# New lists for every queue of a fused attention and gMLP kernel: another order of the last early x, and other distances between scores, maximum and shift

## The chip, the cores and the metric

The kernel runs on one core of one Trainium2 chip. A time is device microseconds of one execution; of several runs the median is given. The core has five engines that work beside each other, each strictly through its own queue: TensorE (PE, with its weight loads PEld), VectorE (DVE), ScalarE (ACT), GpSimd (POOL) and SyncE (SP), which here issues nearly all transfers. They wait for each other through semaphores only.

## The reference

```python
def _attn_ref(q, k, v, tau):              # (8, 8, 576, 64) each
    scale = 1.0 / np.sqrt(q.shape[-1])
    scores = scale * np.matmul(q, k.transpose(0, 1, 3, 2))
    thresh = np.max(scores, axis=-1, keepdims=True) - tau
    scores = np.where(scores >= thresh, scores, -1000000000.0)
    scores = scores - np.max(scores, axis=-1, keepdims=True)
    attn = np.exp(scores)
    attn = attn / (np.sum(attn, axis=-1, keepdims=True) + 1e-09)
    return np.matmul(attn, v)

def _moe_ref(x, w_in, w_spatial, b_spatial, w_out):    # x: (8, 576, 512)
    h = np.maximum(x @ w_in, 0.0)
    u, v = h[..., :512], h[..., 512:]
    v_n = (v - mean(v)) / np.sqrt(var(v) + 1e-06)      # over the last axis
    v_s = np.einsum('ts,bsd->btd', w_spatial, v_n) + b_spatial[None, :, None]
    return (u * v_s) @ w_out
```

The attention of all heads is laid side by side as x and goes through the gMLP. Only scores within tau = 0.02 of their row's maximum keep a weight.

## The kernel before

**Steps.** The 64 heads form 32 pairs of two heads of one batch. The 576 rows of a pair are four blocks of 128 and one of 64; the two blocks of 64 of neighbouring pairs share a step. That gives 18 steps a batch and 144 in all. Step g uses bank g % 2 of the two score banks `s_ring`, slot g % 3 of `e_ring`, g % 10 of `p_ring` and g % 12 of `pT_ring`. So the scores of step g + 2 cannot start before the exponentials of step g have left the bank.

**Tokens.** Nothing chooses the order while the kernel is built: `ORDER` holds one list of tokens for each of eight rounds, `LAST` four short lists for the end. `run_token` reads them one by one and emits each one's instructions. Since every engine takes its own in order, a list fixes five queues at once; the order between two tokens of different engines matters only by what their data needs. `S14:0` is step 14 of the round's own batch; `:1` means the batch before, `:2` two before, `:-1` the next.

One step, with the line where each works and its engine:

- `S` (`scores`, line 817, PE): most of the scores. `G` (`turn_bank`): an empty instruction that waits for one of them, on GpSimd, or on ScalarE (`aG`) or VectorE (`vG`). `Y` (`scores_end`, PE): the rest of the scores, which waits for `G`.
- `M` (`top`, line 851, DVE): the row maximum of both heads. `B` (`shift`, line 857, DVE): it becomes a bias that has tau in it.
- `E`, `F` (`spread`, lines 872 and 875, ACT): one head each, out of the bank.
- Then the step's way in `WAYS`. Way a: `E` and `F` give the shifted scores, with those below the threshold driven far down, and `Z` (`exps`, line 910, ACT) the exponential of both heads. Way n: `E` and `F` give the exponential, `C` (`keep`, line 894, DVE) the mask and `A` (`pick`, line 903, DVE) the masked numerator.
- `T` (`turn_p`, line 915, SP): a DMA transpose of the numerators p into pT.

Other tokens: `Pmjk` (PE) is one step's product of pT and v, three of them fill a bank; `imj` (line 532, DVE) takes the reciprocal of the sums and `pmj` (line 535, DVE) writes x. `X0` and `X1` (`send_x`, line 556, SP) transpose the x of two pairs by DMA into xT; `XP` and `xp` do it on TensorE with an eviction. `v`, `u`, `s`, `o` (lines 643, 710, 739, 768, PE) are the gMLP's products and `ev`, `bv`, `eu`, `es`, `eo` evict them; `bs` and `ba` or `n` and `k` make statistics, `N` the norm (lines 683 to 695, GpSimd); `OUT` (lines 700 and 787) stores. `QA`, `QB`, `QR` transpose q and k on PE, `qa`, `qb`, `qr` evict them, `kd`, `sq`, `sv` copy on GpSimd, `L` loads. A `d` ahead of an eviction puts it on VectorE instead of ScalarE.

```python
        elif kind in ("X", "XR"):
            send_x(m, 4 if kind == "XR" or 2 * m in x_on_pe else 0, 5 if kind == "XR" else 9)
```

**The end.** After round 7 the score banks are given up for six more banks, and `LAST[1]` finishes batch 6's gMLP and batch 7's attention. `X0:1` there sends the early x of batch 7, from its steps 0 to 8; the late x goes through `XP2` and `XP3`. Then `last_gmlp` runs batch 7's gMLP: its first products (line 935) need all of xT; bn_stats (line 944), the norm, the gate (line 983) and the output (line 1002) follow. `LAST[2]` and `LAST[3]` put its u products between.

Of the kernel before, what the change touches and what calls it, by code (L numbers as in the profile page):

```python
# [11 lines left out]
F16 = mybir.dt.float16  # L12
# [8 lines left out]
    "S0:0 L8:0 aG0:0 Y0:0 QA1:0 qa1:0 L6:-1 M0:0 S1:0 G1:0 Y1:0 QR1:0 L7:0 B0:0 F0:0 sk1:0 M1:0 B1:0 E0:0 "  # L21
    "QB1:0 C0:0 S2:0 A0:0 qb1:0 Cb0:0 aG2:0 E1:0 Y2:0 M2:0 B2:0 F1:0 Z1:0 S3:0 dqr1:0 G3:0 Y3:0 F2:0 E2:0 "
    "L4:-1 sv0:0 QR2:0 kd1:0 S4:0 G4:0 M3:0 Y4:0 B3:0 E3:0 F3:0 Z3:0 S5:0 C2:0 G5:0 Y5:0 sq2:0 QA2:0 A2:0 "
    "Ci1:0 M4:0 B4:0 M5:0 E4:0 F4:0 S6:0 B5:0 C4:0 vG6:0 E5:0 A4:0 F5:0 Y6:0 S7:0 G7:0 M6:0 Z5:0 Y7:0 qr2:0 "
    "sv1:0 sq3:0 QB2:0 B6:0 T0:0 kd2:0 M7:0 F6:0 E6:0 Cbs0:0 S8:0 B7:0 vG8:0 qa2:0 E7:0 F7:0 dqb2:0 Y8:0 "
    "RP01:0 M8:0 Z6:0 S9:0 vG9:0 Y9:0 T2:0 B8:0 F8:0 C7:0 E8:0 L1:-1 QR3:0 rp01:0 S10:0 G10:0 qr3:0 M9:0 "
    "L3:-1 Y10:0 B9:0 E9:0 kd3:0 F9:0 RP00:0 Cis1:0 A7:0 M10:0 L0:-1 T1:0 Z8:0 S11:0 sq0:-1 vG11:0 L9:0 T3:0 "
    "T6:0 B10:0 F10:0 Y11:0 QB3:0 drp00:0 M11:0 QA3:0 E10:0 S12:0 Co0:0 qb3:0 G12:0 Y12:0 T5:0 C9:0 qa3:0 "
    "B11:0 QB0:-1 F11:0 A9:0 sq1:-1 E11:0 M12:0 S13:0 G13:0 Y13:0 B12:0 P000:0 P001:0 C11:0 M13:0 B13:0 T7:0 "
    "P002:0 Z10:0 A11:0 F12:0 E12:0 S14:0 qb0:-1 aG14:0 Y14:0 P010:0 M14:0 P011:0 i00:0 F13:0 Cs1:0 B14:0 "  # L30
    "E13:0 S15:0 p00:0 Css2:0 G15:0 Y15:0 P012:0 Z12:0 QR0:-1 M15:0 i01:0 B15:0 T8:0 E14:0 F14:0 sv3:0 S16:0 "
    "dqr0:-1 G16:0 T9:0 Z14:0 L7:-1 T11:0 F15:0 sv2:0 p01:0 Y16:0 kd0:-1 QA0:-1 M16:0 P020:0 E15:0 Z13:0 "
    "P021:0 S17:0 C15:0 B16:0 dqa0:-1 aG17:0 Y17:0 E16:0 P100:0 P022:0 A15:0 T10:0 F16:0 Z16:0 M17:0 "),
(
    "S0:0 i02:1 G0:0 B17:1 Y0:0 P101:1 p02:1 M0:0 Ci0:1 F17:1 P102:1 RP11:1 i10:1 Cis0:1 E17:1 S1:0 B0:0 "
    "Cos0:1 Z17:1 T14:1 G1:0 Y1:0 p10:1 drp11:1 WS2:1 E0:0 F0:0 QB1:0 S2:0 ws2:1 G2:0 M1:0 Y2:0 QA1:0 B1:0 "
    "E1:0 T12:1 C0:0 L2:0 Css3:1 dqb1:0 F1:0 M2:0 qa1:0 RP10:1 S3:0 G3:0 B2:0 T16:1 Y3:0 QR1:0 rp10:1 A0:0 "
    "P110:1 P111:1 F2:0 dqr1:0 M3:0 P112:1 kd1:0 T15:1 E2:0 S4:0 vG4:0 Y4:0 Z1:0 B3:0 i11:1 P120:1 p11:1 M4:0 "
    "L9:0 T17:1 P121:1 B4:0 F3:0 P122:1 E3:0 S5:0 G5:0 Y5:0 i12:1 XP1:1 Z2:0 p12:1 M5:0 E4:0 XP0:1 F4:0 L5:0 "
    "L8:0 S6:0 sq2:0 xp1:1 XR0:1 aG6:0 B5:0 Y6:0 QB2:0 dxp0:1 sv0:0 F5:0 Ci2:1 Cis2:1 Ci3:1 M6:0 E5:0 Z3:0 "  # L40
    "XP3:1 S7:0 G7:0 dqb2:0 Y7:0 B6:0 XP2:1 dxp2:1 M7:0 L1:-1 B7:0 xp3:1 Cis3:1 QA2:0 T1:0 E6:0 v0:1 F6:0 "
    "Cs0:1 Z4:0 S8:0 XR1:1 dqa2:0 G8:0 bv0:1 bs0:1 Y8:0 QR2:0 sq3:0 F7:0 dqr2:0 M8:0 v1:1 kd2:0 E7:0 ba0:1 "
    "B8:0 C6:0 S9:0 Z5:0 ev1:1 G9:0 Y9:0 v2:1 L3:-1 F8:0 M9:0 Co1:1 A6:0 B9:0 v3:1 E8:0 Css1:1 S10:0 vG10:0 "
    "bv2:1 bv3:1 C8:0 n1:1 Y10:0 QA3:0 bs3:1 Css0:1 F9:0 E9:0 T2:0 M10:0 WS0:1 S11:0 G11:0 L4:-1 T0:0 Y11:0 "
    "Z7:0 T5:0 T7:0 B10:0 dws0:1 qa3:0 N0:1 M11:0 F10:0 E10:0 QB3:0 u3:1 A8:0 qb3:0 S12:0 G12:0 Y12:0 B11:0 "
    "eu3:1 QR3:0 C10:0 bs2:1 Z9:0 u1:1 F11:0 dqr3:0 M12:0 A10:0 kd3:0 E11:0 u0:1 B12:0 deu0:1 S13:0 k1:1 "
    "aG13:0 eu1:1 sv1:0 Y13:0 v4:1 F12:0 P000:0 M13:0 B13:0 ba2:1 E12:0 bv4:1 T6:0 P001:0 P002:0 E13:0 F13:0 "
    "S14:0 vG14:0 i00:0 Y14:0 p00:0 P020:0 P021:0 T8:0 Cos1:1 P022:0 ba3:1 Cs2:1 Css4:1 T3:0 M14:0 Z11:0 "
    "i02:0 S15:0 G15:0 Y15:0 L0:-1 B14:0 RP00:0 L2:-1 p02:0 E14:0 N3:1 M15:0 F14:0 drp00:0 RP01:0 Z13:0 S16:0 "
    "G16:0 Y16:0 QR0:-1 bs4:1 rp01:0 dqr0:-1 B15:0 WS3:1 Z12:0 sq0:-1 M16:0 ws3:1 P010:0 E15:0 P011:0 P012:0 "  # L50
    "ba4:1 T9:0 QB0:-1 N2:1 Co2:1 i01:0 p01:0 B16:0 F15:0 C14:0 WS1:1 dqb0:-1 E16:0 T10:0 S17:0 aG17:0 kd0:-1 "
    "A14:0 N1:1 Y17:0 QA0:-1 ws1:1 N4:1 M17:0 u2:1 T12:0 F16:0 qa0:-1 T11:0 WS4:1 deu2:1 "),
(
    "S0:0 G0:0 Y0:0 QR1:0 B17:1 Z16:1 dws4:2 M0:0 L7:0 F17:1 E17:1 s1:2 B0:0 es1:2 S1:0 G1:0 Y1:0 sq1:0 Z15:1 "
    "T14:1 qr1:0 E0:0 F0:0 s0:2 Z17:1 M1:0 B1:0 sv3:1 S2:0 T13:1 G2:0 Y2:0 u4:2 es0:2 E1:0 F1:0 M2:0 eu4:2 "
    "QB1:0 B2:0 T16:1 S3:0 sv2:1 qb1:0 G3:0 Y3:0 QA1:0 L8:0 E2:0 F2:0 s2:2 M3:0 qa1:0 T15:1 B3:0 P110:1 kd1:0 "
    "C1:0 S4:0 es2:2 A1:0 G4:0 Y4:0 P111:1 Z0:0 E3:0 F3:0 M4:0 T17:1 L1:-1 sq2:0 P100:1 P112:1 B4:0 S5:0 G5:0 "
    "Y5:0 Cos2:2 P101:1 P102:1 i11:1 p11:1 M5:0 P120:1 T0:0 Z3:0 P121:1 P122:1 E4:0 i10:1 L6:0 F4:0 B5:0 Z2:0 "
    "F5:0 S6:0 G6:0 p10:1 i12:1 Y6:0 L5:0 E5:0 QB2:0 p12:1 sq3:0 Z4:0 M6:0 s3:2 B6:0 S7:0 E6:0 F6:0 Co3:2 "
    "dqb2:0 G7:0 Y7:0 Cos3:2 L9:0 Z5:0 es3:2 QA2:0 XR0:1 XP1:1 S8:0 G8:0 T1:0 M7:0 Y8:0 B7:0 dxp1:1 qa2:0 "  # L60
    "QR2:0 dqr2:0 E7:0 F7:0 X1:1 XP2:1 o3:2 M8:0 kd2:0 xp2:1 C7:0 XP0:1 xp0:1 B8:0 F8:0 T4:0 deo3:2 S9:0 E8:0 "
    "L3:-1 A7:0 G9:0 Z6:0 Y9:0 v0:1 sv1:0 T5:0 S10:0 M9:0 G10:0 B9:0 Y10:0 ev0:1 v2:1 v1:1 C8:0 F9:0 M10:0 "
    "sv2:0 E9:0 bv2:1 T2:0 A8:0 S11:0 B10:0 bv1:1 E10:0 G11:0 n0:1 Y11:0 C9:0 QB3:0 sv0:0 bs2:1 F10:0 bs1:1 "
    "v3:1 qb3:0 Z10:0 QA3:0 S12:0 ba2:1 bv3:1 M11:0 G12:0 Y12:0 QR3:0 ba1:1 B11:0 A9:0 N2:1 M12:0 qa3:0 F11:0 "
    "L0:-1 qr3:0 B12:0 u2:1 E11:0 kd3:0 F12:0 o0:2 E12:0 S13:0 eu2:1 bs3:1 sv3:0 vG13:0 deo0:2 Y13:0 S14:0 "
    "G14:0 Y14:0 s4:2 M13:0 B13:0 T3:0 o1:2 es4:2 T8:0 v4:1 T10:0 T7:0 Z12:0 deo1:2 k0:1 E13:0 F13:0 Z11:0 "
    "S15:0 sq0:-1 N0:1 M14:0 G15:0 bv4:1 Y15:0 ba3:1 L8:-1 u3:1 P000:0 B14:0 P001:0 E14:0 M15:0 P002:0 eu3:1 "
    "F14:0 P010:0 P011:0 P012:0 T6:0 L4:-1 bs4:1 i00:0 N1:1 B15:0 F15:0 E15:0 p00:0 i01:0 QB0:-1 S16:0 G16:0 "
    "L7:-1 p01:0 Y16:0 OUT1:2 u0:1 dqb0:-1 T12:0 ba4:1 QR0:-1 M16:0 deu0:1 S17:0 L9:-1 Z14:0 B16:0 Z13:0 "
    "aG17:0 Y17:0 QA0:-1 qr0:-1 T13:0 N3:1 P020:0 P021:0 M17:0 N4:1 E16:0 qa0:-1 B17:0 P022:0 F16:0 s0:1 "  # L70
    "kd0:-1 C15:0 "),
(
    "S0:0 F17:1 E17:1 Z16:1 T14:1 G0:0 Y0:0 i02:1 S1:0 A15:1 T11:1 L2:0 p02:1 es0:2 M0:0 Z17:1 G1:0 B0:0 Y1:0 "
    "u1:2 X0:1 E0:0 o2:3 T9:1 deu1:2 sq1:0 F0:0 QA1:0 M1:0 sq2:0 S2:0 eo2:3 B1:0 aG2:0 dqa1:0 F1:0 Y2:0 s1:2 "
    "M2:0 B2:0 T16:1 QR1:0 E1:0 es1:2 dqr1:0 Z0:0 OUT3:3 S3:0 G3:0 T15:1 E2:0 Y3:0 T17:1 QB1:0 qb1:0 M3:0 "
    "L0:-1 s2:2 es2:2 s3:2 B3:0 kd1:0 es3:2 Z1:0 P100:1 P101:1 P102:1 F2:0 sq3:0 i10:1 S4:0 G4:0 Y4:0 p10:1 "
    "E3:0 T1:0 F3:0 S5:0 aG5:0 Y5:0 OUT4:3 M4:0 B4:0 P120:1 P121:1 P110:1 M5:0 Z3:0 P111:1 L6:0 P122:1 P112:1 "
    "i12:1 E4:0 F4:0 S6:0 G6:0 L5:0 Y6:0 B5:0 C4:0 p12:1 i11:1 p11:1 M6:0 Z2:0 F5:0 E5:0 o1:2 o0:2 B6:0 S7:0 "
    "G7:0 F6:0 deo1:2 L8:-1 eo0:2 Y7:0 A4:0 QB2:0 o2:2 E6:0 T0:0 L3:-1 qb2:0 sv0:0 M7:0 eo2:2 B7:0 QR2:0 X1:1 "
    "S8:0 L1:-1 qr2:0 G8:0 C5:0 Y8:0 C6:0 QA2:0 T4:0 E7:0 F7:0 qa2:0 v0:1 bv0:1 A5:0 M8:0 T3:0 B8:0 kd2:0 "  # L80
    "S9:0 vG9:0 Y9:0 v1:1 E8:0 F8:0 A6:0 Z7:0 ev1:1 bs0:1 S10:0 M9:0 B9:0 G10:0 F9:0 Y10:0 v3:1 OUT1:2 ba0:1 "
    "v2:1 T6:0 M10:0 C8:0 E9:0 B10:0 C9:0 sv1:0 T7:0 bv3:1 bv2:1 F10:0 sv3:0 S11:0 E10:0 G11:0 Y11:0 A9:0 "
    "u4:2 s4:2 eu4:2 M11:0 sq0:-1 es4:2 A8:0 QB3:0 Z10:0 S12:0 aG12:0 qb3:0 B11:0 F11:0 Y12:0 N0:1 QR3:0 "
    "bs2:1 dqr3:0 E11:0 Z11:0 QA3:0 dqa3:0 T5:0 kd3:0 v4:1 S13:0 G13:0 Y13:0 o3:2 M12:0 B12:0 M13:0 bv4:1 "
    "T2:0 sq1:-1 bs4:1 E12:0 u1:1 sv2:0 B13:0 F12:0 eo3:2 T10:0 S14:0 F13:0 G14:0 Y14:0 deu1:1 P000:0 E13:0 "
# [85 lines left out]
(  # L171
    "u2:1 eu2:1 u3:1 eu3:1 u4:1 eu4:1 ")]
WAYS = [
    "nananaanananaaanaa",
    "naaaaanananaaanaaa",
    "anaaaaannnaaaaanaa",
    "aaaannnannaaaaanaa",
    "aaaaaanaannnaannaa",
    "nnaaannanaanaanaaa",
    "nnaaaanaananaaanaa",  # L180
    "nnaaaanananaaaaaaa",
]

# [1028 lines left out]
```

## Time and profile before

| what | value |
|---|---|
| median of 3 runs | 444.53 us (441.93 to 445.1) |
| the profiled execution | 442.4 us |
| its span, first to last instruction | 440.6 us |
| mean granted TensorE clock | 0.99 |
| PE, DVE, ACT, POOL busy | 412.2, 381.6, 383.1, 169.4 us |
| maxima (line 851) | 144, 1.361 us each |
| E and F (lines 872, 875) | 288 in all, 0.74 us each |
| exponentials of way a (line 910) | 97, 1.172 us each |
| mask and pick of way n (lines 894, 903) | 47, 0.487 and 0.799 us |
| pT transposes (line 915), xT transposes (line 556) | 141 and 15; median to landing 4.4 and 4.8 us |

How to read it: busy is the time in which an engine has at least one instruction in it, so overlapping instructions count once. A matmul's end is modelled, so a PE that is busy all the time still has short waits between groups. A line such as "A <- B: 16.3, 33, 1.4" says that A waited 16.3 us for B in total, 33 times, at most 1.4. The chain of waits goes back from the last instruction to whatever released each one. In the table by stretches, each engine's busy time is followed by its count, then come the granted clock, the share of the DMA engines and GB/s.

### The profile page before, as it was taken

What the parts mean: (1) busy time and instruction counts of PE and PEld (TensorE: products, weight loads), DVE (VectorE), ACT (ScalarE), POOL (GpSimd) and SP (SyncE); (2) the same over time, 40 slices, a digit from 0 to 9 for tenths busy, and PEclk for the clock granted to TensorE, in tenths of its full rate; (3) what the DMA queues carried; (4) which work ended last, traced back from release to release, by engine and by line L of the source; (5) the groups of instructions that cost most, each with busy time, mean ns of one, the idle gap of its engine ahead of it and who ended that gap; (6) DMA issues with size and microseconds to landing.
All of it is one profiled execution on the core that took longest, in us unless ns stands there. A gap on an engine that the chain in (4) does not pass through costs nothing.

```text
span 440.6 us, 12956 instructions
## 1 busy us (share of the span) xinstructions
PE 412.2 (94%) x5048; PEld 256.7 (58%) x5048; DVE 381.6 (87%) x693; ACT 383.1 (87%) x579; POOL 169.4 (38%) x374
## 2 busy tenths in 40 slices
PE   8778888989999999999999999999999999999695
PEld 4445664666656665666665565656656656556352
DVE  6889988898998989998899899889999999995472
ACT  4899999989999888999998998898999988997252
POOL 2254335474346511661137612362155521361021
PEclk9899999999999999999999999999999999999899
DMA  7999999999999999999899999999999997978803
GB/s 199 228 241 214 219 274 190 196 214 209 240 179 239 207 224 230 219 172 207 202 213 187 211 229 189 219 264 235 192 186 188 206 238 152 182 163 135 191 12 109
DMA packets 224637, 88.17 MB, mean 200 GB/s; under 512 B 195648, under 2 KB 220352, under 8 KB 224576
## 3 DMA queue, kind: packets, MB, share of 16 engines
q1 hardware_dynamic: 224048, 86.49, 99.8%
q8 instruction: 40, 0.66, 0.7%
q0 software_dynamic: 160, 0.52, 0.3%
q10 hardware_dynamic: 368, 0.33, 0.2%
q14 instruction: 21, 0.17, 0.2%
HBM read 32.79 MB, written 9.44 MB: 96 GB/s over the span
## 4 chain that ended last, share of the span: by engine, by line
PE 57%; DVE 15%; ACT 13%; DMA 6%; issue 4%; POOL 2%; SPq 0%; POOLq 0%; DVEq 0%; ACTq 0%
PE s L817 23%; DVE s L851 8%; PE f L739 6%; PE f L643 5%; ACT e L875 5%; PE f L497 4%; PE f L710 4%; PE f L435 4%; DMA xT<-xn 4%; PE f L768 3%; ACT p L910 3%; ACT e L872 3%; PE f L492 1%; DVE p L903 1%; DVE xn L535 1%
## 5 line engine op out<-in xcount | busy, mean ns | idle before, releaser
L851 DVE TENSOR_REDUCE s<-s 128x2 f32<-128x1152 f32 x144 | 196.0, 1361 | 17.8 <-PE s L817 15.8
L817 PE MATMUL s<-qkT 64*64 64x160 f32 (+1 forms) x2304 | 173.0, 418 | 10.5 <-ACT e L875 5.3
L817 PEld LDWEIGHTS s<-qkT 64*64 64x64 f32 x2304 | 107.3, 132 | 69.7 <-ACT e L875 16.3
L875 ACT ACTIVATE e<-s,negm 128x576 f32<-128x576 f32 x194 | 134.4, 743 | 10.5 <-DVE negm L857 7.0
L910 ACT ACTIVATE p<-e 128x1152 f16<-128x1152 f32 x97 | 112.5, 1172 | 1.5 <-PE s L817 1.0
L872 ACT ACTIVATE e<-s,negm 128x576 f16<-128x576 f32 x94 | 65.2, 745 | 8.9 <-DVE negm L857 7.6
L321 POOL CAST v<-vl 128x512 bf16<-128x512 f32 x32 | 21.9, 685 | 65.9 <-PE s L817 64.7
L497 PE MATMUL f<-v,pT 128*128 128x65 bf16 x984 | 44.1, 194 | 0.0
L497 PEld LDWEIGHTS <-pT 128*128 128x128 f16 x1024 | 41.8, 98 | 2.0 <-issue 0.5
L903 DVE TENSOR_TENSOR p<-e 128x576 int32<-128x576 int32 x47 | 37.5, 799 | 1.1 <-PE s L817 0.8
L294 POOL COPY qn<-ql 128x512 f32<-128x512 f32 x31 | 20.6, 663 | 42.6 <-PE s L817 42.2
L447 POOL COPY qkT<-qkT 64x64 f32<-64x64 f32 x32 | 8.7, 272 | 67.8 <-ACT qkT L417 33.4
L739 PE MATMUL f<-wsT,vn 128*128 128x512 bf16 x135 | 32.9, 380 | 0.2 <-POOL vn L695 0.2
L710 PE MATMUL f<-xT,w_in 128*128 128x512 bf16 x116 | 29.6, 380 | 0.1
L643 PE MATMUL f<-w_in,xT 128*128 128x512 bf16 x112 | 28.0, 380 | 1.3 <-DMA xT<-xn 1.1
L695 POOL TENSOR_SCALAR vn<-vrel,rs,nm 128x512 bf16<-128x512 f32 (+1 forms) x35 | 27.2, 777 | 3.6
L492 PE MATMUL f<-v,pT 128*128 128x130 bf16 x123 | 27.3, 222 | 1.1 <-DMA pT<-p 0.6
L535 DVE TENSOR_TENSOR xn<-f,r 128x384 bf16<-128x384 f32 x46 | 25.4, 554 | 0.9 <-PE s L817 0.2
L768 PE MATMUL f<-w_o,gT 128*128 128x512 bf16 x100 | 25.4, 380 | 0.3 <-DVE qkT L411 0.2
L857 DVE TENSOR_SCALAR negm<-s 128x2 f32<-128x2 f32 x144 | 22.3, 155 | 3.5 <-PE s L817 0.6
L894 DVE TENSOR_SCALAR e<-e 128x1152 uint16<-128x1152 f16 x47 | 22.8, 487 | 0.3 <-PE s L817 0.2
L739 PEld LDWEIGHTS <-vn 128*128 128x128 bf16 x140 | 12.8, 98 | 15.4 <-issue 2.0
(162 smaller groups left out, 548.4 us busy)
## 6 DMA issues: line engine op xcount, KB each, us to landing
vl<-in_v_dram SPq DMA_DIRECT2D x16, 512.0 KB, 5.6
kl<-in_k_dram SPq DMA_DIRECT2D x15, 512.0 KB, 4.9
ql<-in_q_dram SPq DMA_DIRECT2D x15, 512.0 KB, 5.2
out_dram<-oo SPq DMA_DIRECT2D x12, 512.0 KB, 4.3
pT<-p SPq DMA_TRANSPOSE x141, 4.4
uT<-in_moe_w_in_dram SPq DMA_DIRECT2D x3, 512.0 KB, 5.3
uT<-in_moe_w_spatial_dram SPq DMA_DIRECT2D x2, 576.0 KB, 5.5
vx<-in_v_dram SPq DMA_DIRECT2D x16, 64.0 KB, 4.2
```

The costliest lines, as they stand in the source:

```text
L492: nc.tensor.matmul(out=t[:, at:at + 130], lhsT=pt[:, 4, rows], rhs=vt[:, 4:6, :].rearrange("p b d -> p (b d)"), start=True, stop=False)
L497: nc.tensor.matmul(out=t[:, at + 65 * h:at + 65 * h + 65], lhsT=pt[:, 5 * h + j, rows], rhs=vt[:, 6 * h + j, :], start=False, stop=(h == 1 ...
L643: nc.tensor.matmul(out=t, lhsT=x_of(b, f, slice(c * P, (c + 1) * P)), rhs=w_in[:, f, 512:1024], start=(f == 0), stop=(f == 3))
L710: nc.tensor.matmul(out=t, lhsT=w_in[:, m, f * P:(f + 1) * P], rhs=x_of(b, m, slice(0, 512)), start=(m == 0), stop=(m == 3))
L739: nc.tensor.matmul(out=t, lhsT=vn[:, c, f * P:(f + 1) * P], rhs=wsT[:, c, 0:512], start=(c == 0), stop=(c == 4))
L768: nc.tensor.matmul(out=t[:n], lhsT=gs[b][:, f, c * P:c * P + n], rhs=w_o[:, f, :], start=(f == 0), stop=(f == 3))
L817: made.append(nc.tensor.matmul(out=s_ring[g % 2][halves[k], at[h] + lo:at[h] + hi], lhsT=qks[n][halves[h], 0, m:m + 64], rhs=qks[n][halves ...
L851: nc.vector.tensor_reduce(out=nm[:, heads], in_=view(s_ring[g % 2], at[h0], dims), axis=AX.X, op=ALU.max, negate=True)
L872: nc.scalar.activation(out=half_e(g)[0][:, S * h:S * h + S], in_=s, func=ACT.Exp, bias=bias_, scale=scale if steps[g][1] == 4 else 1.0)
L875: nc.scalar.activation(out=e, in_=s, func=ACT.Prelu, bias=bias_, scale=scale if steps[g][1] == 4 else 1.0, alpha=1e30)
L903: nc.vector.tensor_tensor(out=numerators(g).bitcast(I32), in0=e.bitcast(I32), in1=kept.bitcast(I32), op=ALU.bitwise_and)
L910: nc.scalar.activation(out=numerators(g), in_=e_ring[g % 3].rearrange("p h s -> p (h s)"), func=ACT.Exp)
```

## The change

All eight lists of `ORDER`, `LAST[0]` and `LAST[1]`, and five of the eight strings of `WAYS` are replaced. No function changes. The number of tokens of each kind stays, but for these:

- One more step goes way n (48 instead of 47), 96 instead of 97 way a. In the last batch step 0 leaves way n, and steps 15 and 17 join it.
- Evictions on VectorE: `eo` 11 (13 before), `qa` 7 (10), `qr` 11 (13), `rp` 2 (3), `ws` 3 (2), `xp` 4 (3).
- Relays `G`: GpSimd 114 (109), ScalarE 11 (18), VectorE 19 (17).
- Seven blocks of v make their statistics on ScalarE (`n`, `k`) as before, but three of them are other blocks.

In the tail the stores before `X0:1` change: `OUT3:3` goes to `LAST[0]`, `T10:1` comes into `LAST[1]`, and `X0:1` stands before `XP3`. The order of the products changes little, `P100` moves up, `o2` stands before `P022`. The file has one line less, so that the kernel's functions stand one line higher (816 for 817 and so on).

Of the diff, the ends of the last round's list and all that follows:

```diff
--- before.py
+++ after.py
...
-    "G14:0 M13:0 i01:0 B13:0 ev4:1 Y14:0 o2:2 N3:1 p01:0 E13:0 F13:0 M14:0 B14:0 deo2:2 u1:1 S15:0 Z12:0 n4:1 "
-    "aG15:0 Y15:0 F14:0 deu1:1 T6:0 T9:0 M15:0 u0:1 E14:0 OUT1:2 T10:0 B15:0 S16:0 N0:1 bs1:1 k4:1 aG16:0 "
-    "Y16:0 eu0:1 o3:2 N4:1 M16:0 F15:0 E15:0 Z14:0 ba1:1 u2:1 S17:0 Z13:0 deo3:2 T12:0 vG17:0 Y17:0 B16:0 "
-    "u3:1 F16:0 N1:1 eu3:1 deu2:1 s1:1 M17:0 B17:0 s0:1 F17:0 ")]
...
+    "C10:0 B12:0 qb3:0 v4:1 P010:0 Z11:0 S13:0 aG13:0 Y13:0 bs1:1 P011:0 P012:0 A10:0 sv2:0 F12:0 E12:0 N0:1 "
+    "M13:0 ev4:1 B13:0 S14:0 G14:0 Y14:0 o2:2 n4:1 i01:0 p01:0 T8:0 T11:0 M14:0 B14:0 u1:1 F13:0 E13:0 ba1:1 "
+    "deo2:2 Z12:0 S15:0 bs3:1 G15:0 F14:0 Y15:0 u0:1 E14:0 M15:0 S16:0 k4:1 aG16:0 eu1:1 Y16:0 o3:2 eu0:1 "
+    "OUT4:2 B15:0 E15:0 u2:1 F15:0 ba3:1 eo3:2 S17:0 T12:0 T6:0 M16:0 vG17:0 deu2:1 B16:0 Z13:0 Y17:0 T9:0 "
+    "u3:1 N1:1 Z14:0 N4:1 M17:0 N3:1 eu3:1 s0:1 B17:0 es0:1 s1:1 F17:0 ")]
 LAST = [(
-    "T8:1 es1:2 E17:1 es0:2 s3:2 T11:1 "),
+    "C15:1 es1:2 OUT3:3 A15:1 E17:1 T13:1 s3:2 "),
 (
-    "OUT4:3 E16:1 s2:2 T13:1 P020:1 P021:1 es3:2 Z16:1 T14:1 sv3:1 P022:1 i02:1 P100:1 u4:2 es2:2 P110:1 "
-    "P111:1 P112:1 Z15:1 T16:1 P101:1 o3:2 Z17:1 T15:1 i11:1 o1:2 P102:1 p02:1 i10:1 P120:1 T17:1 p11:1 s4:2 "
-    "eu4:2 P121:1 P122:1 eo3:2 p10:1 i12:1 XP2:1 o2:2 p12:1 xp2:1 XP3:1 xp3:1 o0:2 OUT3:3 es4:2 X0:1 deo1:2 "
-    "eo2:2 eo0:2 "),
+    "s2:2 es3:2 P020:1 P100:1 E16:1 C17:1 P021:1 T10:1 P110:1 es2:2 u4:2 P111:1 F16:1 T14:1 P112:1 A17:1 o2:2 "
+    "P022:1 Z16:1 P101:1 P102:1 i10:1 i02:1 o1:2 T15:1 s4:2 P120:1 T16:1 i11:1 p02:1 T17:1 p11:1 deu4:2 eo2:2 "
+    "P121:1 p10:1 P122:1 o3:2 i12:1 p12:1 XP2:1 X0:1 XP3:1 xp3:1 xp2:1 eo1:2 o0:2 eo3:2 es4:2 deo0:2 "),
...
@@ -174,11 +173,11 @@
     "nananaanananaaanaa",
     "naaaaanananaaanaaa",
     "anaaaaannnaaaaanaa",
-    "aaaannnannaaaaanaa",
-    "aaaaaanaannnaannaa",
-    "nnaaannanaanaanaaa",
-    "nnaaaanaananaaanaa",
-    "nnaaaanananaaaaaaa",
+    "aaaannnanaaaaaanaa",
+    "aaaaaannannnaanaaa",
+    "anaaannannanaanaan",
+    "anaaaanaananaaanan",
+    "anaaaanananaaaanan",
 ]
```

The other seven lists are replaced in the same way.

## The prediction

> **What bounds the kernel now.** I read, in order, the page's busy shares and slices, the busy table for each batch, the waits, the chain of waits near the end, and the busy table around its last long gap.
>
> ```profile
> span 440.6 us, 12956 instructions
> ...
> PE 412.2 (94%) x5048; PEld 256.7 (58%) x5048; DVE 381.6 (87%) x693; ACT 383.1 (87%) x579; POOL 169.4 (38%) x374
> ...
> PE   8778888989999999999999999999999999999695
> ...
> DVE  6889988898998989998899899889999999995472
> ACT  4899999989999888999998998898999988997252
> ```
>
> Three engines are full for nine tenths of the span, and all three fall off in the last slices. The execution took 442.4 us: its span of 440.6 and 1.8 around it.
>
> The stretches of two batches, cut at the first maximum of a batch:
>
> ```profile
> core 0: us, PE busy (x) PEld busy (x) DVE busy (x) ACT busy (x) POOL busy (x), PEclk, DMA share, GB/s
> 7.40:49.30 41.90, 33.06 (x436) 22.00 (x432) 38.22 (x61) 37.45 (x54) 15.85 (x37) 0.96 1.14 231
> ...
> 302.20:350.80 48.60, 48.16 (x638) 30.94 (x634) 45.85 (x81) 46.04 (x72) 19.73 (x44) 1.00 1.10 206
> ...
> sum 389.60, PE 372.20 PEld 234.03 DVE 357.07 ACT 361.53 POOL 162.46; mean PE 46.52 PEld 29.25 DVE 44.63 ACT 45.19 POOL 20.31
> ```
>
> From the first maximum (7.4) to the last (397.0) the 144 steps take 389.6 us, 2.72 each. ScalarE idles 28.1 of it, VectorE 32.5, and from the third batch on TensorE about 1 us a batch or less. So a new order has little to win here: a few us, not tens. What it can win is unevenness:
>
> ```profile
> PEld s L817 <- ACT e L875: 16.3, 33, 1.4
> DVE s L851 <- PE s L817: 15.8, 40, 1.2
> ...
> PEld s L817 <- ACT e L872: 11.6, 25, 1.2
> ```
>
> 58 times the scores waited until the exponentials two steps back had left their bank, and 40 times the maximum waited for the scores: one loop through three engines, at most 1.4 us at a time.
>
> The end is different. The chain of waits there:
>
> ```profile
> 408.30 0.61 DVE ql L779
> 408.92 0.35 SPq L783
> 409.33 0.42 SPq L787
> 409.80 5.52 DMA xT<-xn
> 415.37 3.22 PE t L935 x8
> ```
>
> The transfer of the early x of batch 7 (token X0) stands last on SP, behind the store of an output that VectorE copies at 408.30 and behind another store of 512 KB. It lands at 415.3, and only then may the last gMLP (line 935) begin. Around that gap:
>
> ```profile
> 412.00:415.40 3.40, 0.03 (x1) 0.03 (x2) 0.82 (x2) 0.58 (x1) 0.00 (x0) 0.89 1.22 180
> 415.40:422.00 6.60, 6.60 (x28) 2.56 (x29) 3.52 (x10) 3.03 (x6) 0.37 (x1) 0.80 0.20 75
> ```
>
> TensorE does nothing for 3.4 us, and the granted clock then averages 0.80: the first six matmuls of line 935 start 427 ns apart, the later ones 216.
>
> **Part 1, X0 at the end.** I lay the new lists on the old times from the last maximum on (M17, which ends at 398.63 before). Its surroundings keep their pace: the last norm on GpSimd (N1 before, N3 now; 0.20+0.58+0.27+0.78 = 1.8 us by lines 683 to 695) still ends near 398, where the four s products begin. They take TensorE to 402.3.
>
> VectorE: es0 needs the first s product, so it ends at 399.9 as before; then C15 (0.49 by line 894), es1 (0.68), A15 (0.80, line 903) to 401.8, es3, C17, es2 to 403.6, A17 to 404.4. Two steps of the last batch changed from way a to way n, so ScalarE loses two exponentials (1.17 each by line 910) and VectorE gains 2 x 1.29. The engine was idle there for 1.25 us at one reciprocal and 1.72 at another, which hides most of it. ScalarE then has only Z16 left, ready at 402.7. The last three p's come at 401.8, 402.7, 404.4; before, they came at 402.0, 403.0, 404.2. That is no gain.
>
> SP: T10 has moved into the tail, one issue of about 1.3 us, where SP idled from 400.3 to 402.1, so it costs nothing. T15, T16 and T17 follow each other at 1.3 us and are issued by about 406; before, a slow issue of 2.3 us held T17 until 405.9.
>
> TensorE: P020, P100, P021, P110 (0.31 each), u4 (0.47), P111, P112, o2 (0.87), P022, P101, P102 run from 402.3 to 406.6. The evictions are in order on VectorE, and i10 stands ahead of i02, so P102 gates them: i10, i02, i11 (0.15 each apart) and p02 (0.55) end at 407.8. The store ahead of X0 is now copied by ScalarE at about 406 and does not hold it. **X0 is issued at 407.85 instead of 409.80: 1.95 earlier.**
>
> How long it then takes is not shown. The fifteen xT transfers took 3.3 to 6.6 us, median 4.8; this one 5.5, just behind the 512 KB store, which now goes before T13. I take 4.8, so that it lands at 412.65: 2.7 earlier. With 5.5 it is 2.0; and no more than 3.4 can be had, since the other work of TensorE (o1, s4, P120 to P122, o3, XP2, XP3, o0: 4.7 us from 406.6) reaches 411.3, and XP3's eviction 411.9.
>
> **The clock.** The row: a gap of 3.41 us was followed by 3.4 us at half clock, while the 1.17 us gap before the scores at 29.35 was not (clock 1.00). The Trainium skill (TensorE: Matmul & The Clock Gate, "What's actually happening") says that the clock halves after an idle window of about 3.4 us, and that the window runs free. The new gap, 411.3 to 412.7, is 1.4 us, so by the rule the clock stays. Line 935's four groups then take 0.86 us each, and the fifth bn_stats (0.69, with 0.38 behind it: 1.07 apart) starts 6.0 us after the first matmul instead of 7.1. Row and rule together give 1.1 us; if the clock fell all the same, 0. Were the gap 3.0 us, the row alone would not tell.
>
> Behind it the code is the same instruction for instruction. **Tail: 2.7 + 1.1 = 3.8 us gained**, between 0 (an unseen wait takes X0's place) and 3.4 + 1.1 = 4.5.
>
> **Part 2, the eight lists.** Sums first, from both kernels' tokens and the rows' durations. Of the evictions, eight go from VectorE to ScalarE and two the other way, 0.27 to 0.69 us each (lines 409 to 417), and one step more goes way n (1.17 off ScalarE, 1.29 onto VectorE). ScalarE gets 1.8 us more, VectorE 2.4 less, TensorE the same; they have 28 and 32 us idle in the steps to hide it. In 40% of the steps (58 of 144) the scores wait for ScalarE, so I charge 0.4 x 1.8 = 0.7.
>
> Then evenness. I add the list's work of VectorE between one maximum and the next, from the second batch on. Before, 21 steps have over 3.5 us, 10.5 us over it in total; now 15 steps, 7.1 over. ScalarE's steps over 3.5 go from 29 (17.4 over) to 24 (13.3). The trace shows what a heavy step costs: the heaviest, 5.0 us of list work in the last batch, took 4.8 us, the next 1.5: together 6.3 against 5.4 for two mean steps. Some 0.4 of its excess stays. 0.4 x 3.4 = 1.4 us gained.
>
> The tokens between a maximum and its shift grow from 34.8 to 40.5 us of VectorE work. This would lengthen the loop by up to 5.7 us. But in the trace ScalarE idled 0.12 us before the exponentials of steps that have such work, 0.15 of those without: I charge 0. Relays (G) leave ScalarE (18 to 11), and go to GpSimd (109 to 114) and VectorE (17 to 19): nothing where the queue is empty. Loads from HBM move by some steps on SP; before, waits for them show on GpSimd alone, at most 3.9 us, and TensorE's longest wait for GpSimd is 1.5: 0.
>
> **Steps: 1.4 - 0.7 = 0.7 us gained**, with ends of +3.5 and -4: one tenth of the idle time of the engines either way.
>
> **Sum.** 3.8 + 0.7 = 4.5 us: 442.4 becomes 437.9. The median of the runs shown is 444.53, 2.1 above the profiled execution, so the median becomes 440.0.
>
> **Rivals.**
>
> - A new wait takes X0's place. For: p02 stands behind i10 and so behind P102, and A17 ends late on VectorE; XP3's eviction and the PE queue end by 411.9 in any case. If X0 is issued only 0.5 us earlier, or the steps lose the 3 us that the tail wins, 1 to 3 us remain: about 442.5. Against: A17 ends 2.8 us before p02 starts, and the store's copy over 1 us before X0.
> - The relay becomes the bound, and the kernel gets slower. Five more relays stand on GpSimd. It works in order, so a relay behind a norm waits up to 1.8 us, and with it the second part of the scores (Y), on an engine that has no idle time from batch 2 on. Each full catch costs up to 1.8 us. Five cost 9.1, take back the 4.5 and leave 4.6 more: 449. It decides from about five on. For: the shares of TensorE. Against: in the trace GpSimd waits for the scores (64.7 us before line 321), not the reverse, and is 38% busy.
> - The change does not do what it says: T10 and the copies hold SP, X0 is issued at 409.8 as before, and the lists are equal. 444.5.
>
> **Numbers.** Likeliest case 0.50 (faster by over 1%, which is about what a measurement of this kernel can tell from no change); a new wait, or no effect, 0.38 (within 1%); relays or lists that fit worse 0.12 (slower). Range: the gain of both parts at their ends, 4.5 + 3.5 = 8, and the scatter of the median, 1, give 435.5; the other side takes in the second and third rivals and some of the slow one, 446.
>
> **What would show it.** Right: X0 issued about 9 us after the last maximum ends, landing 14 us after it (16.7 before); a TensorE gap before the last gMLP near 1.4 us; all its matmuls 216 ns apart; about 389 us between first and last maximum. Wrong: a gap of 3 us again, or a stretch over 393 us; waits of line 816's weights for GpSimd would show the relay.

## The result, and the profile after

| | before | after |
|---|---|---|
| median | 442.0 us (438.68 to 446.12, 22 runs) | **438.99 us** (436.27 to 442.31, 22 runs) |
| ratio, 95% interval | | **0.9932 (0.9909 to 0.9955)** |
| the profiled execution | 442.4 us | 439.63 us |
| its span | 440.6 us | 437.9 us |
| start to first maximum (line 851, now 850) | 7.64 us | 8.15 us |
| first to last maximum | 389.6 us | 390.2 us |
| end of the last maximum to the end of the span | 42.0 us | 38.1 us |

The kernel is 3.0 us faster (0.68% of 442.0). The two profiled executions differ by 2.8 us, and the last three rows add up to it: 0.5 lost at the start, 0.6 lost in the steps, 3.9 gained in the tail. The first two are within the scatter: in the profiles of e5 and e6 below, which have the same lists in the steps, these took 389.5 and 389.0 us, and in those of e1 and e4, with the old ones, 387.9 and 389.0. So all of the gain that is clear of it lies behind the last maximum.

The page of the new kernel, its first lines and its slices of TensorE, VectorE and ScalarE:

```profile
span 437.9 us, 12915 instructions
...
PE 406.9 (93%) x4998; PEld 257.2 (59%) x5048; DVE 376.3 (86%) x689; ACT 383.5 (88%) x584; POOL 168.6 (39%) x374
...
PE   8778889989999999988999999999999999999895
...
DVE  6889989898989889987889898988998998998482
ACT  4899989999999988998988999999999989998252
```

VectorE is busy 5.3 us less in the span and ScalarE 0.4 more. The slice in which TensorE fell to 6 stands at 8 now.

The stretches of batches, cut at each batch's first maximum (busy time of each engine with its count; first batch, seventh batch and the sum of all eight):

```profile
8.15:50.05 41.90, 33.30 (x454) 22.78 (x452) 37.96 (x61) 38.05 (x55) 14.67 (x35) 0.96 1.06 225
...
303.33:352.19 48.86, 47.79 (x627) 31.04 (x634) 45.23 (x82) 45.88 (x70) 19.86 (x46) 1.00 1.11 214
...
sum 390.22, PE 368.32 PEld 234.84 DVE 349.60 ACT 363.91 POOL 163.01; mean PE 46.04 PEld 29.35 DVE 43.70 ACT 45.49 POOL 20.38
```

VectorE lost 7.5 us of work in the steps (357.07 to 349.60) and ScalarE got 2.4 more (361.53 to 363.91), in the direction that the tokens gave; VectorE's part is larger than the 2.4 of the sum in part because C15, A15, C17 and A17 stand behind the last maximum now. The stretch did not get shorter. The waits tell the same story, those of the loop and those of TensorE for pT and for the relay:

```profile
DVE s L850 <- PE s L816: 18.7, 45, 0.9
PEld s L816 <- ACT e L874: 18.1, 36, 1.0
...
PEld s L816 <- ACT e L871: 15.2, 32, 1.7
...
PEld L491 <- DMA pT<-p: 4.9, 6, 1.7
...
PEld s L816 <- POOLq L831: 0.2, 1, 0.2
```

The waits of the loop grew: the scores waited 33.3 us for exponentials (27.9 before), the maximum 18.7 us for scores (15.8 before). TensorE waited 4.9 us for pT (1.1 before), a wait that the sum did not have. VectorE's saved work became idle time.

The end, from the chain of waits:

```profile
408.33 0.34 DVE r L531 x3
408.67 0.44 issue
409.22 4.91 DMA xT<-xn
414.18 1.05 PE t L934 x4
```

The early x of batch 7 is now held by the reciprocal i02 and its p02, no longer by a copy and two stores. Counted from the end of the last maximum, it is issued after 9.5 us (11.2 before) and the last gMLP starts after 14.4 (16.7 before). TensorE around the gap:

```profile
414.18 2.12 PE L934 MATMUL t<-w_in,xT 128*128 128x512 bf16 x9 [1.20 <-DMA xT<-xn]
```

The gap is 1.2 us instead of 3.4, and the clock stays up behind it, by the row of the stretch around the gap; the second and third line are the fifth bn_stats before and now:

```profile
411.00:420.00 9.00, 7.78 (x45) 3.44 (x45) 6.14 (x17) 4.98 (x9) 0.86 (x1) 1.00 0.35 109
...
422.47 0.68 DVE L944 BATCH_NORM_STATS2 st<-o 64x6 f32<-64x512 f32 x1
...
420.05 0.68 DVE L943 BATCH_NORM_STATS2 st<-o 64x6 f32<-64x512 f32 x1
```

From the first matmul of the last gMLP to that bn_stats it is 5.87 us now and was 7.10.

### The profile page after: what moved, and what is told of

It is laid out like the page before. It is cut to its first block, busy times and chain, and to the rows that moved or that the text cites. A ratio compares the mean times of both kernels' runs of the same rounds, so it can differ in the third digit from the quotient of the medians.

```text
span 437.9 us, 12915 instructions
## 1 busy us (share of the span) xinstructions
PE 406.9 (93%) x4998; PEld 257.2 (59%) x5048; DVE 376.3 (86%) x689; ACT 383.5 (88%) x584; POOL 168.6 (39%) x374
## 4 chain that ended last, share of the span: by engine, by line
PE 64%; ACT 12%; DVE 8%; DMA 6%; issue 5%; POOL 4%; SPq 1%; POOLq 0%; ACTq 0%; DVEq 0%
PE s L816 27%; PE f L738 6%; ACT e L874 5%; PE f L434 5%; PE f L496 5%; DVE s L850 5%; PE f L709 4%; PE f L642 4%; PE f L767 4%; DMA pT<-p 3%; ACT e L871 2%; ACT p L909 2%; PE f L491 2%; DMA xT<-xn 1%; PE f L627 1%
## 5 line engine op out<-in xcount | busy, mean ns | idle before, releaser
L850 DVE TENSOR_REDUCE s<-s 128x2 f32<-128x1152 f32 x144 | 196.2, 1362 | 22.3 <-PE s L816 18.7
L871 ACT ACTIVATE e<-s,negm 128x576 f16<-128x576 f32 x96 | 66.8, 746 | 6.4 <-DVE negm L856 4.5
L320 POOL CAST v<-vl 128x512 bf16<-128x512 f32 x32 | 20.2, 632 | 78.3 <-PE s L816 66.1
L694 POOL TENSOR_SCALAR vn<-vrel,rs,nm 128x512 bf16<-128x512 f32 (+1 forms) x35 | 28.4, 812 | 3.6
L709 PE MATMUL f<-xT,w_in 128*128 128x512 bf16 x100 | 28.6, 380 | 1.3 <-ACT qkT L414 0.3
L642 PE MATMUL f<-w_in,xT 128*128 128x512 bf16 x103 | 27.1, 380 | 0.5
L687 POOL TENSOR_TENSOR rs<-rs,mhalf 128x1 f32<-128x1 f32 (+1 forms) x35 | 21.2, 607 | 2.9
```

Of the source, the lines that this page charges most:

```text
L642: nc.tensor.matmul(out=t, lhsT=x_of(b, f, slice(c * P, (c + 1) * P)), rhs=w_in[:, f, 512:1024], start=(f == 0), stop=(f == 3))
L709: nc.tensor.matmul(out=t, lhsT=w_in[:, m, f * P:(f + 1) * P], rhs=x_of(b, m, slice(0, 512)), start=(m == 0), stop=(m == 3))
L850: nc.vector.tensor_reduce(out=nm[:, heads], in_=view(s_ring[g % 2], at[h0], dims), axis=AX.X, op=ALU.max, negate=True)
L871: nc.scalar.activation(out=half_e(g)[0][:, S * h:S * h + S], in_=s, func=ACT.Exp, bias=bias_, scale=scale if steps[g][1] == 4 else 1.0)
```

## Experiments

The theory: the change gains only through X0 at the end, by its earlier landing and by the clock that then stays up; the eight lists add a little because their work is more even. The rivals: the lists do nothing, or the relays that went to GpSimd cost something. All kernels were compared with the kernel before; a ratio below 1 is faster. The new lists are the kernel after, the old lists the kernel before.

### e1: one token alone

The old lists, with X0 of batch 7 moved up in `LAST[1]`:

```diff
-    "... P120:1 T17:1 p11:1 ... o0:2 OUT3:3 es4:2 X0:1 deo1:2 eo2:2 eo0:2 "
+    "... P120:1 T17:1 X0:1 p11:1 ... o0:2 OUT3:3 es4:2 deo1:2 eo2:2 eo0:2 "
```

> The kernel before with one token moved: X0:1 of the last list stands right behind T17:1, ahead of the two stores. If the landing of the last early x is what the change gains by: X0 issued at about 407.2 instead of 409.8, landing near 412, TensorE's gap under 1 us, the clock at 1.0 through line 935, and 3.5 us less than before (ratio 0.992). If the gain comes from the eight lists, 0 to 1 us less (0.998 or more).

Measured: 436.73 us, ratio 0.9891 (0.9852 to 0.9931). X0 is issued at 407.23 and lands at 410.57; the last gMLP starts at 412.01. The end of the chain there (old line numbers):

```profile
410.43 0.59 PE f L768 x2
411.03 0.28 PE t L577 x5
411.31 0.86 PE t L768 x4
412.17 0.88 PE t L935 x4
```

No xT transfer stands in it any more: TensorE's own queue (o0 and the transposes of XP3) sets the start. One token moved does about as much as all lists made anew, and likely more; the two intervals overlap (0.9852 to 0.9931 here, 0.9909 to 0.9955 there).

### e2: the new end alone

The old rounds 0 to 6, then the new round 7, `LAST` and last string of `WAYS`. Where the two meet, round 7 takes over what the old round 6 leaves open:

```diff
-    "S0:0 G0:0 ... sq2:0 F17:1 ... A17:1 ..."
+    "S0:0 C15:1 B17:1 p10:1 G0:0 ... sq1:0 sq2:0 F17:1 ... Z17:1 ..."
```

> Rounds 0 to 6 of the kernel before, round 7, the four last lists and the last string of ways of the changed one (five tokens are placed by hand at the seam). If the end makes the gain and the other rounds nothing: 3 us less than before (0.993), with last maximum to last instruction near 39.6 us (43.4 before). If the rounds make it: under 1 us less.

Measured: 438.88 us, ratio 0.9937 (0.9917 to 0.9957), which is the whole change. From the end of the last maximum the span has 38.5 us left, against 42.0 and 38.1 (the expectation counts from its start, where it is 39.8 against 43.4).

### e3: the new rounds alone

The new rounds 0 to 6, then the old round 7 and `LAST`:

```diff
-    "S0:0 C15:1 ... Z17:1 ..."
+    "L6:0 S0:0 C15:1 ... C17:1 A17:1 ..."
```

> The opposite: rounds 0 to 6 of the changed kernel, round 7 and the end of the one before. If the rounds are worth the 0.7 us forecast: ratio 0.998. If they cost as the profile after lets one think (0.6 us in the steps and 0.5 ahead of them): 1.002 to 1.003. If they are what gains: 0.993.

Measured: 442.54 us, ratio 1.0018 (0.9989 to 1.0048); 390.6 us from first to last maximum. The interval allows a gain of at most 0.5 us and a loss of 2.1. The 0.7 us of the prediction's second part are not there, at least not in these seven of the eight lists.

### e4: the gap filled

The old lists, with twelve matmuls on constants where TensorE waits for X0; nothing uses their output:

```diff
+        t = bank()
+        for _ in range(12):
+            nc.tensor.matmul(out=t.rearrange("p (a b) -> p a b", a=4), lhsT=warm,
+                             rhs=warm.unsqueeze(1).broadcast_to([P, 4, P]), start=True, stop=True)
         rest = last_gmlp(Z)
```

> The kernel before with twelve matmuls more on ones (line 1149's form, 216 ns each at full clock) between the last output of batch 6 and the last gMLP, where TensorE stood idle for 3.4 us. X0 still lands at 415.3. If the slow clock behind the gap costs what was forecast: clock 1.0 and 1.1 us less than before (0.9975). If the clock is not on the path: no change, or slower if the filling delays line 935.

Measured: 440.27 us, ratio 0.996 (0.9938 to 0.9982), so 1.8 us (0.8 to 2.7) for the filling. Its stretch behind the landing:

```profile
414.10:420.00 5.90, 5.85 (x30) 2.50 (x32) 3.80 (x13) 3.60 (x7) 0.87 (x1) 1.00 0.22 84
```

X0 is issued as late as ever, 11.2 us after the last maximum ends, but the clock is 1.00 behind it instead of 0.80, and the fifth bn_stats starts 5.9 us after the first matmul of line 935 instead of 7.1. These 1.2 us are the clock's. The tail is 1.7 us shorter in this profile; the other 0.5 lie in the flight, which took 5.03 us here and 5.52 in the profile of before (5.32 in e3's, with the same end), so that they are scatter as far as is known.

### e5: X0 late again

The new lists, X0 put back behind the copy `eo3`:

```diff
-    "... XP2:1 X0:1 XP3:1 xp3:1 xp2:1 eo1:2 o0:2 eo3:2 es4:2 deo0:2 "
+    "... XP2:1 XP3:1 xp3:1 xp2:1 eo1:2 o0:2 eo3:2 X0:1 es4:2 deo0:2 "
```

> The changed kernel with X0:1 moved back behind the stores of the last outputs (behind eo3:2). If X0's landing is what sets the end: X0 issued near 414, landing near 418.5, a gap of 5 us or more ahead of the last gMLP, the half clock behind it, and 5 to 6 us more than the changed kernel: ratio to the kernel before 1.005 to 1.008. If the rest of the new order makes the gain: 0.993 as without the move.

Measured: 444.82 us, ratio 1.0067 (1.0043 to 1.0091). The chain of waits:

```profile
413.67 3.42 DMA xT<-xn
417.08 0.05 issue
417.13 6.54 PE t L934 x16
```

The gap is 5.0 us, and sixteen matmuls of line 934 take 6.54 us, 0.41 each: half the clock, and nearly twice what they take at 0.22. This one token is worth some 6 us (1.0067 against 0.9932), more than the whole change.

### e6: X0 earlier still

The new lists, with i02 and p02 right behind P022 so that they don't stand behind i10, and X0 right behind T17:

```diff
-    "... o2:2 P022:1 Z16:1 P101:1 P102:1 i10:1 i02:1 o1:2 ... i11:1 p02:1 T17:1 p11:1 ... XP2:1 X0:1 XP3:1 ..."
+    "... o2:2 P022:1 i02:1 p02:1 Z16:1 P101:1 P102:1 i10:1 o1:2 ... i11:1 T17:1 X0:1 p11:1 ... XP2:1 XP3:1 ..."
```

> The changed kernel with i02 and p02 right behind P022 (ahead of i10) and X0:1 right behind T17 (ahead of the store of o2). If p02 waiting for P102 and the store are what is left in X0's way: X0 issued at the end of T17's issue (8.5 us after the last maximum ends instead of 9.5), landing within 3.5 to 4.9 us, the gMLP then bound by TensorE's own queue, and 1.2 us less than the changed kernel: ratio to the kernel before 0.990. If TensorE's queue was already the bound: 0.993.

Measured: 436.84 us, ratio 0.9892 (0.9865 to 0.9919). X0 is issued at 406.99, lands at 410.25, and the gap is gone:

```profile
410.28 0.28 PE t L576 x5
410.56 0.86 PE t L767 x4
411.42 0.88 PE t L934 x4
```

### e7: all relays on GpSimd

The new lists, every `aG` and `vG` turned into `G` (30 more relays on GpSimd):

```diff
-    "... vG6:0 ... aG8:0 ... vG12:0 ... aG13:0 ... aG16:0 ... vG17:0 ..."
+    "... G6:0 ... G8:0 ... G12:0 ... G13:0 ... G16:0 ... G17:0 ..."
```

> The changed kernel with all 144 relays on GpSimd, 30 more than it has. If a relay behind a norm holds the scores (the rival): up to 1.8 us for each one caught; with a third of the 30 caught by half of that, 9 us more, ratio to the kernel before 1.013. If relays cost nothing where the engine idles 60% of the time: 0.993 as without the edit.

Measured: 446.75 us, ratio 1.0138 (1.0089 to 1.0186), so 9 us over the new lists (its one profile is 6.5 longer than theirs: 1.2 in the steps, 5.6 in the tail, the start 0.4 shorter). Two places show it. The scores waited for relays, mostly in the second batch, which took 53.5 us (50.3 in the new lists' profile, but 51.9 in e5's with the same lists):

```profile
PEld s L816 <- POOLq L831: 6.7, 8, 1.9
```

And at the end the relay of step 17 stands ahead of the last norms on GpSimd. The timeline of GpSimd, and the s products that wait for the norms:

```profile
391.29 0.18 POOL L669 TENSOR_SCALAR nmean<-sm 64x1 f32<-64x1 f32 x1
398.57 0.19 POOL L682 TENSOR_SCALAR rs<-mv 128x1 f32<-128x1 f32 x1 [7.10 <-PE s L816]
...
404.87 3.54 PE L738 MATMUL f<-wsT,vn 128*128 128x512 bf16 x9 [3.57 <-POOL vn L694]
```

The norms that the new lists start at 392.5 start at 398.6, behind a relay that waited 7.1 us for scores; the s products, the gate and all behind them come later (43.7 us from the last maximum to the end instead of 38.1). TensorE idles for 3.57 us ahead of them, and its clock is 0.50 from 405.4 to 408.8, which is part of the loss. So a relay on GpSimd can cost far more than the rival allowed. In the new lists themselves it does not: there TensorE waited for a relay there once, 0.2 us.

### e8: VectorE relieved

The new lists, bn_stats of the gMLP over 64 of 512 columns in batches 0 to 6; the variance there is that of these columns alone:

```diff
-            nc.vector.bn_stats(out=st[:n], in_=hold["vrel"][:n])
+            nc.vector.bn_stats(out=st[:n], in_=hold["vrel"][:n, 0:64])
```

> The changed kernel with bn_stats on 64 of the 512 columns in rounds 1 to 7 (the variance is then taken over these columns alone; the last gMLP is left as it is), which takes some 0.55 us from VectorE 28 times, 15 us in all. If VectorE's load in the steps bounds them, as the step on evenness supposed: several us less, ratio to the kernel before 0.975 to 0.985. If TensorE and ScalarE set the pace of the steps: within 1 us of the changed kernel, 0.991 to 0.994.

Measured: 437.54 us, ratio 0.992 (0.9885 to 0.9954), as the new lists. The row from first to last maximum, new lists first:

```profile
8.15:398.37 390.22, 368.32 (x4629) 234.84 (x4674) 349.60 (x610) 363.91 (x552) 163.01 (x361) 1.00 1.04 210
```

```profile
7.42:396.71 389.29, 371.21 (x4675) 234.50 (x4676) 338.01 (x609) 364.39 (x552) 162.92 (x361) 1.00 1.05 211
```

VectorE has 11.6 us less to do, and the stretch is 0.9 us shorter: 10.7 us became idle time. The 0.9 is itself within the scatter (389.0 to 390.2 us in the three profiles of the new steps).

### e9: TensorE relieved

The new lists, three of the five products in each sum of the spatial part, in batches 0 to 6:

```diff
-                for c in range(5):
+                for c in range(3):
...
-                                     rhs=wsT[:, c, 0:512], start=(c == 0), stop=(c == 4))
+                                     rhs=wsT[:, c, 0:512], start=(c == 0), stop=(c == 2))
```

> The new lists, with three of the five products in each sum of the gMLP's spatial part (token s, lines 726 to 740 of the changed kernel; batches 0 to 6): two fifths of the terms are left out, and the output of those batches with them. It takes eight full matmuls of 0.216 us and eight of 64 columns from TensorE per batch, about 2 us a batch, 12 in the steps and 2 in the tail. If TensorE's queue is what paces the steps, most of the 12 come off: 0.965 to 0.975 of before, and the stretch between first and last maximum falls to 380. If the loop of scores, maximum and exponentials paces them, the work becomes idle time as VectorE's 15 us did in e8: 0.988 to 0.993, stretch 388 to 390.

Measured: 436.52 us, ratio 0.9886 (0.9839 to 0.9934). The row of the steps:

```profile
7.87:397.03 389.16, 360.12 (x4534) 228.17 (x4578) 348.63 (x609) 364.04 (x552) 162.85 (x361) 1.00 1.06 210
```

TensorE's busy time fell by 8.2 us there (12 expected), the stretch by 1.1. The 1.1 is within the same scatter; by the runs it is 2 us (0.9886 against 0.9932), with intervals that overlap. An engine that is busy for 94% of the stretch, and that I had called full, does not pace it alone either.

### e11: ScalarE relieved, VectorE loaded

As e8, with twelve more steps on way n, two in each of batches 1 to 6; `C` and `A` stand where `Z` stood. For one of them:

```diff
-    "... p11:1 p12:1 Y6:0 M6:0 o0:2 Z2:0 E5:0 A4:0 F5:0 ..."
+    "... p11:1 p12:1 Y6:0 M6:0 o0:2 C2:0 A2:0 E5:0 A4:0 F5:0 ..."
```

> The new lists as in e8 (bn_stats over 64 of 512 columns, so that the variance is that of these columns alone), and twelve more steps on way n, two in each of batches 1 to 6: C and A stand where the exponential Z stood. ScalarE loses 12 x 1.17 = 14 us; VectorE gets 12 x 1.29 = 15.5 us in place of the 15 that e8 took from it, so it carries what it carries in the new lists. If ScalarE paces the steps, most of the 14 come off against e8: 0.965 to 0.975, stretch near 380. If TensorE or the loop does, 0.990 to 0.997, stretch 388 to 391. Were VectorE's place in the loop what counts, it would be slower than e8, about 1.00.

Measured: 450.09 us, ratio 1.0194 (1.0171 to 1.0218). The row of the steps, and two waits of ScalarE (lines one higher, 903 is the pick A):

```profile
7.59:410.51 402.92, 372.97 (x4629) 236.73 (x4674) 351.84 (x633) 352.30 (x540) 167.03 (x361) 0.99 1.01 203
```

```profile
ACT e L875 <- DVE negm L857: 12.7, 20, 2.3
ACT e L872 <- DVE p L903: 6.5, 2, 4.6
```

ScalarE has 12.1 us less than in e8 and VectorE 13.8 more, which brings it to what it carries in the new lists. Yet the steps take 13.6 us more than in e8 and 12.7 more than in the new lists. The waits name two reasons: the shift came late behind C and A on VectorE (F waited 12.7 us for it, 5.7 in e8), and E waited for a pick (twice, up to 4.6 us) that had to free its slot of `e_ring` first. It was the case that I had put last, and the size was missed: about 1.00 expected. Two stretches of 3.4 us at half clock, from 97.2 and 175.7 behind gaps of 1.96 and 2.86 us on TensorE, belong to the 13.6 with at most 1.7 each. Since these waits came with the relief, the run does not tell what a lighter ScalarE alone would bring.

### e10: both best parts

The old rounds 0 to 6 as in e2, with the end of e6.

> The old lists of rounds 0 to 6 (as in e2) with the new end in which i02 and p02 stand behind P022 and X0 behind T17 (as in e6). The theory that end and rounds add up: e2 0.9937, and e6 gained 0.0040 on the new lists, so 0.990; if the small loss of the new rounds (1.0018 in e3) is real too, 0.987 to 0.990. If the end's gain depends on what the rounds before leave over: 0.993 or more.

Measured: 437.42 us, ratio 0.9911 (0.9888 to 0.9934); steps 388.6 us, tail 37.0. It agrees with the sum of the parts. e1, e6 and e10 can't be told from each other by their intervals. e6 is faster than the kernel before by its interval; against the new lists that is likely and not certain (its upper end, 0.9919, lies below their 0.9932, but inside their interval). Its direct reason is that no gap is left at the last gMLP.

## Why the prediction was right, and where it was not

Forecast: a gain of 4.5 us, 440.0 us. Measured: 3.0 us, 438.99 us. The forecast of the time came so close because the median of the runs shown stood 2.5 us above the one measured beside the new kernel; the gain itself was forecast at one and a half times what was measured. So the nearness of the two times is in part luck. The case called likeliest, over 1% faster, did not come: the measured 0.68% (0.45 to 0.91) lies within 1%, which had 0.38. Nor was 1% what can be told from no change: with 22 runs of each kernel 0.7% stands clear of it.

- **X0's walk: right.** Foreseen was the issue 9.2 us after the last maximum ends, the landing after 14.0, a gap of 1.4. It is 9.5, 14.4, 1.2. P102 gates i10, i02 and p02 as foreseen, and the store ahead holds nothing. The landing is 2.3 us earlier and not 2.7: the row of reciprocals ended 0.3 later, and the flight took 4.9 us against 4.8.
- **The clock: right in size, but its rule is too narrow.** Its term was 1.1 us; the profiles show 1.2 (5.87 us now, 7.10 before), and e4, which fills the gap and leaves the lists alone, 1.8 (0.8 to 2.7). The Trainium skill (TensorE: Matmul & The Clock Gate, "What's actually happening") gave the idle window that counts as about 3.4 us, running free; gaps of 1.2 and of 3.41 fell on the two sides of it here. But the trace of before already had 3.4 us at half clock, from 15.3 to 18.7, behind gaps of at most 1.00 us, and other profiles behind gaps of 1.6 to 2.9 (last section). The measured gap of 1.2 kept its clock, and so did those of 0.8 to 1.3 at the same place in e2, e7, e9 and e11; that a gap must last 3.4 us is not so here.
- **A term that was not in the sum.** 0.35 us were gained between the fifth bn_stats and the end, all in the last semaphore instructions on GpSimd. In all kernels here with the new rounds the last gMLP takes 0.3 us less from there to the end, whatever their end was; why is open. With the two terms above that makes the tail's 3.9 us. That the sum had 3.8 is luck in part: the landing gave 0.4 less, and this term makes it up.
- **ScalarE's charge of 0.7: the direction holds, the size is not shown.** Scores wait 5.4 us more for exponentials. What that costs was not tried alone, and the steps' 0.6 us are within the scatter.
- **Evenness, 1.4 us: not seen, and most likely the step that failed.** Its input was right: by the durations in the two traces VectorE's excess over 3.5 us between two maxima, from the second batch on, fell from 10.0 to 6.5 us (10.5 to 7.1 in the sum). The price, 0.4 of it, came from two steps of one batch. e3 has seven of these lists and gains at most 0.5 us in total, so either the price was too high or ScalarE's charge too low; no run tells these two apart. e8 takes 11.6 us off the same engine (the excess falls to 4.3) for 0.9 us that are within the scatter: the sum of VectorE's work does not pace the steps. e11 shows what can: the same sum of VectorE in another place, ahead of a shift or as a pick that frees a slot, went with 13.6 us more. Work counts by what waits behind it, and the sum I made doesn't see that.
- **"Relays 0": right for these lists, and e7 shows that the rival had a real price.** Its 449 was foreseen from five caught relays; thirty moved relays made 9 us, and the larger part (5.6 of the 6.5 in the profile) by a way that it did not name, the norms behind one relay in the tail.
- **The rival that a new wait takes X0's place: partly there.** What holds X0 now is p02 behind i10, as it said; but it comes 1.7 us earlier than the old hold. e6 takes this hold away and gains a further 1.8 us (0.9892 against 0.9932, of 441.6).

The start was not in the sum. The first maximum comes 0.5 us later in the new profile, but in the profiles of all these kernels it lies between 7.4 and 9.6 us, also in those with the same first list (7.5 in e4, 9.6 in e1), so that this is the scatter of one execution.

## What to carry to other kernels

Before an order is made anew, follow the last chain to its one late issue and move that token alone: here it gave about as much as ten new lists, or more. Where three engines in a loop are busy for 90%, the sum of an engine's work is no measure of what relief brings: taking 12 us from VectorE or 8 from TensorE gave about 1 us in the profiles, which is within their scatter, and at most 2 by the runs' medians, while 14 us of VectorE in the wrong place cost 13. And a gap of some us on TensorE is worth closing twice, once for the wait and once for the slow matmuls that may follow it.

## What the runs showed of the hardware that I had not expected

- A gap of 3.41 us lowered the clock in the profile of before, one of 3.57 did in e7 and one of 5.0 in e5, and one of 3.27 in e3's profile did not (clock 1.00 behind it). The length of one gap does not decide: half clock also came behind gaps of 1.75 us (e3), 1.91 (e5), 1.62 (e9), 1.96 and 2.86 (e11), while gaps of 1.65 (e6), 1.56 (e7) and 1.58 (e11) left it at 1.00. In all thirteen stretches at half clock that these profiles have before 430 us, TensorE had been busy for at most half of the 3.4 us right ahead, in one gap or in several. That this share is what counts fits them, but was not tried. The rows of the first one of before, and of the one of e3 with the gap ahead of it:

```profile
11.90:15.30 3.40, 1.59 (x21) 1.01 (x25) 3.01 (x5) 3.18 (x5) 1.20 (x4) 1.00 1.16 262
15.30:18.70 3.40, 3.40 (x30) 2.09 (x31) 2.69 (x5) 2.53 (x3) 0.51 (x1) 0.50 1.22 212
...
57.40:59.15 1.75, 0.03 (x4) 0.00 (x0) 1.72 (x5) 1.46 (x3) 0.00 (x0) 1.00 1.25 65
59.15:62.55 3.40, 3.38 (x41) 2.79 (x43) 1.15 (x4) 1.29 (x2) 0.06 (x1) 0.50 0.95 256
```

- Over all executions the mean granted clock was 0.993 in before and in e3, and 0.996 in the new lists, e1, e2 and e4. One stretch of 3.4 us at half clock is worth 0.0039 of a span of 440 us, so by this estimate the old gap brought it in some 70% of executions, if half clock elsewhere is as frequent in all of them. Part of the scatter goes with it: of the 78 executions of before that were timed beside e1 to e8, the 32 with a mean clock of 0.995 or more had a median of 440.7 us, the others one of 442.5.
- The flight of the same xT transfer took 3.26 to 3.34 us in the three profiles in which no store stood right ahead (e1, e6, e10), and 5.0 to 5.5 in the three behind a store of 512 KB (before, e3, e4). Behind one of 256 KB it took anything from 3.2 to 4.9 us (e8 3.23, e5 3.42, e9 4.24, e11 4.50, the new lists 4.91, e2 and e7 4.94). I had taken the median of all fifteen; what decides between the values behind the small store stays open.
